# Forty small unread products ahead of the transposes of chunk 4's K, in a delta-rule attention and SwiGLU kernel

## The chip, the cores and the metric

The kernel runs on one core of one Trainium2 chip. The metric is the device time of one execution in microseconds; the time of a kernel is the median of its runs. The profile is of one execution, which has a time of its own and a span, from its first instruction to its last.

## What is computed

Two stages in float32, the second on the output of the first. The attention stage is a delta rule: for each of 4 batches and 8 heads, a 48x48 state is carried over 768 steps.

```
k_n = k / (norm(k) + 1e-6)
for t in range(S):
    y[t]  = q[t] @ state
    v_old = k_n[t] @ state
    state = state + beta[t] * outer(k_n[t], v[t] - v_old)
x   = y, heads side by side          # 3072 tokens x 384
g   = x @ w_gate                     # 384 x 1536
out = (g * sigmoid(g) * (x @ w_val)) @ w_out
```

## The kernel before

The sequence is cut into 12 chunks of 64 steps. Within a chunk the recurrence becomes matrix products: K is transposed (`turned`, from line 485), the products of K with itself and with Q are formed (`gram_steps`, L527), a triangular system is inverted for two chunks at a time (`invert`, `join`, L826 and L838 for the chunks 2 and 3, L921 and L935 for later pairs), and `advance` (L960 to L1212) uses these with the state: L977 and L960 multiply by the state, L1043 applies the inverse, L1145 updates the state, L1133 finishes y, L1206 transposes y for the next stage, and ScalarE copies that to SBUF at L1212. The feed-forward stage of a chunk works on its 256 tokens: gate and value products (L1409 for the chunks 0 and 1, L1313 for later ones, which use a scheme with fewer products), and the output products (L1436, L1519).

The order is written out by hand: all engines are under a manual schedule, and each engine's instructions run in the order in which the program issues them. The feed-forward products of chunk c are interleaved with the steps of the attention stage for chunk c+1: `point(c)` issues the next step of `advance`, or, through `prep_step`, the next preparation. One such preparation is `products(k_c, q_c)` (L1643), a generator of two steps. Its first step issues the transposes of K of chunk k_c and of Q of chunk q_c; its second issues their products. K of the chunks 4 and 5, and Q of chunk 2, are transposed on TensorE (L511, eight 128x128 transposes for each, into the PSUM pair `px` for K and `py` for Q) and copied out by ScalarE (L515). From chunk 6 on VectorE transposes K. The constant `AHEAD` is 4. `products(4, 2)` is issued right after the transposes of y of chunk 1 (L1206), which go to `py`.

There are already two kinds of product whose result nobody reads. `unread` (L651) is a 128x32 by 128x512 product; `small_unread` (L653 to L658) is a 32x32 by 32x1 product, in turn on the four 32-row quadrants. In the kernel before, 48 small ones and two large ones stand at the start, and 16 small ones (to `py`) and some large ones a little later, all before 26 us.

```
def small_unread(count, tag="px"):
    p = banks("p_t", tag)[0]
    for n in range(count):
        q_ = QUADS[n % 4][0]
        nc.tensor.matmul(p[q_, 0:1], half[q_], half[q_, 0:1])
```

In the trace each float32 product has two weight loads and two products, so 48 of these appear as 96 loads (PEld) and 96 products (PE). A transpose has one of each. Whatever TensorE executes is read from its own stream of instructions, which the profile lists as packets of queue q8.

Of the kernel before, what the change touches and what calls it, by code (L numbers as in the profile page):

```python
# [20 lines left out]
def kernel(  # L21
# [74 lines left out]
    AHEAD = 4  # L96
# [379 lines left out]
    def banks(name, tag):  # L476

        if type(tag) is int:
            return [ps_ffn([128, 512], name, tag + i) for i in range(2)]
        p = ps_pair(name, tag)  # L480
        return [p[:, 0], p[:, 1]]
# [3 lines left out]
    def turned(c, of_q, tag=None):  # L485

        if tag is None:
            tag = "py" if of_q else "px"
        x = qpad[c % QB] if of_q else kn_of(c)
        late = c >= blocks_of[of_q][1]  # L490
        if of_q:
            xt_v = qs_v[:, :, :, :, 0:C].rearrange("p b bp j i -> p bp j b i")
        elif late:
            xt_v = kt_of(c).rearrange("p (b bp j i) -> p bp j b i", bp=NB, b=2, j=NJ)
        else:
            xt_v = kt_of(c).rearrange("p (bp j b i) -> p bp j b i", bp=NB, j=NJ, b=2)
        (qt if of_q else kt)[c] = xt_v
        if late:
            blocks = blocks_of[of_q][2].rearrange("p bp h d -> p (bp h d)")
            if of_q:  # L500
                blocks = blocks.rearrange("p (u i) -> p u i", i=C)
            nc.vector.transpose(q_t if of_q else kt_of(c), blocks)
            spent.append(1.8)
            if c + 1 < NCH:
                late_loads.append(lambda: load_blocks(of_q, c + 1))
            return
        p_t = banks("p_t", tag)
        for bp in range(NB):
            for j in range(NJ):
                at = slice(128 * j, 128 * j + 128)  # L510
                nc.tensor.transpose(p_t[bp][:, at], x[:, bp, 2 * j : 2 * j + 2], ident)  # L511
            if type(tag) is int:
                nc.scalar.copy(xt_v[:, bp], p_t[bp].rearrange(P_T, j=NJ, b=2))
        for bp in range(NB if type(tag) is not int else 0):
            nc.scalar.copy(xt_v[:, bp], p_t[bp].rearrange(P_T, j=NJ, b=2))  # L515
        if of_q and c + QB < Q_BLOCKS:
            load_q(c + QB)
# [43 lines left out]
    def gram(*args):  # L561
        for _ in gram_steps(*args):
            pass
# [89 lines left out]
# [6 lines that stand above are left out]
# [983 lines left out]

    def products(k_c, q_c):  # L1643

        if k_c is not None:
            turned(k_c, False)
        if q_c is not None:
            turned(q_c, True)
        yield
        if k_c is not None:  # L1650
            gram(k_c, False, None, (nc.scalar.copy, nc.scalar.copy))
            if k_c % 2 == 1:
                fills.append((k_c // 2, invert(k_c // 2)))
        if q_c is not None and q_c < MERGED:
            gram(q_c, True)
        yield
# [30 lines left out]
    def prep_step(c):  # L1687

        for g in range(1, c // 2 + 2):
            late = g == 1 and (  # L1690
                hold or steps("join", g) >= 2 and steps("advance", 2) < 4
            )
            if g in inverted and steps("join", g) < (4 if g == 1 else 2) and not late:
                step("join", join if g > 1 else join_1, *((g,) if g > 1 else ()))
                return True
        if going:
            next(going.pop())
            return True
        k_c, q_c = None, None
        if q_of and steps("advance", q_of[0] - 1) >= 3:  # L1700
            q_c = q_of.pop(0)
        elif not (c > 0 and hold and not todo and k_ready()):
            return False
        if k_ready():
            k_c = k_of.pop(0)
        gen = products(k_c, q_c)
        next(gen)
        if k_c is not None or q_c < MERGED:
            going.append(gen)
        return True  # L1710
# [210 lines left out]
```

## Time and profile before

| what | value |
|---|---|
| median of 3 runs | 694.35 us (692.88, 694.35, 695.93) |
| profiled execution, its time | 693.74 us |
| profiled execution, its span | 692.0 us |
| TensorE busy (PE) | 676.7 us, 98% of the span, 10756 products |
| weight loads (PEld) | 631.0 us, 91%, 10756 loads |
| VectorE, ScalarE, GpSimdE busy | 60%, 38%, 27% |
| mean granted TensorE clock | 0.995 |
| DMA | 62.23 MB, mean 90 GB/s |

How to read it: "busy" counts a product from its start to its modelled end, so a stream of small products that overlap counts as busy all through. The granted clock is the share of full speed that TensorE was given. In the timeline each row is a group of like instructions: its start in us from the start of the span, its length in us, the engine, the line, the operation, what is written and read, the count, and in brackets how long the engine sat idle before it and what ended that. "issue" in a bracket is idle time in which the engine waited for no other engine and no transfer of data that the profile shows. The chain is the sequence of work that ended last, followed back from the last instruction.

### The profile page before, as it was taken

How to read it: one execution, taken by the hardware profiler on the slowest of the kernel's cores; microseconds unless marked ns; L12 is line 12 of the kernel's file. 1: busy time of each engine (PE TensorE's matmuls, PEld its weight loads, DVE VectorE, ACT ScalarE, POOL GpSimd, SP SyncE). 2: the span in 40 equal slices, each digit the busy share in tenths (PEclk: the TensorE clock that was granted, in tenths of full speed). 3: DMA queues.
4: the chain of work that ended last, by engine and by line, in shares of the span. 5: the costliest groups of instructions: out<-in, count | busy, mean ns of one | idle time of the engine just before them, and what ended most of it. 6: DMA issues, size and time to landing. Idle time of an engine off the chain costs nothing.

```text
span 692.0 us, 24441 instructions
## 1 busy us (share of the span) xinstructions
PE 676.7 (98%) x10756; PEld 631.0 (91%) x10756; DVE 415.8 (60%) x874; ACT 262.7 (38%) x557; POOL 189.9 (27%) x310
## 2 busy tenths in 40 slices
PE   8889999999999999999999999999999999999997
PEld 5777888666999999999899999999999999999997
DVE  7887688897567565637457646655555534433342
ACT  5776765124432522344233245232144242142230
POOL 5110032007880318810036830308810000000000
PEclk9999999999999999999999999999999999999999
DMA  9678733026550611564422364243143121221210
GB/s 138 155 184 223 208 127 103 12 40 182 119 113 15 133 48 41 109 123 69 94 71 71 70 129 81 56 98 82 54 109 69 56 63 47 56 62 46 70 46 23
DMA packets 143849, 62.23 MB, mean 90 GB/s; under 512 B 122976, under 2 KB 126048, under 8 KB 143744
## 3 DMA queue, kind: packets, MB, share of 16 engines
q1 hardware_dynamic: 141536, 60.19, 37.6%
q8 instruction: 84, 1.38, 0.8%
q10 hardware_dynamic: 2080, 0.39, 0.4%
q14 instruction: 21, 0.17, 0.1%
q0 software_dynamic: 128, 0.10, 0.1%
HBM read 53.58 MB, written 7.08 MB: 88 GB/s over the span
## 4 chain that ended last, share of the span: by engine, by line
PE 89%; DMA 4%; ACT 2%; SPq 2%; issue 1%; DVE 1%; POOL 0%; DVEq 0%; POOLq 0%; ACTq 0%
PE ffn L1313 43%; PE ffn L1519 20%; PE ffn L1409 8%; PE ffn L1436 4%; DMA h_f<-in_moe_w_val_dram 2%; PE p_px L977 2%; PE p_py L960 2%; PE p_px L1043 2%; PE p_py L1133 2%; PE p_px L1145 1%; SPq L140 1%; PE p_px L527 1%; PE p_py L1206 1%; PE p_py L935 1%; PE p_px L921 1%
## 5 line engine op out<-in xcount | busy, mean ns | idle before, releaser
L1313 PE MATMUL ffn<-x_ffn,wg_sb 128*128 128x128 f32 x840 | 129.2, 277 | 0.5 <-ACT ffn L1369 0.3
L1313 PE MATMUL ffn<-x_ffn,wv_sb 128*128 128x128 f32 x840 | 128.6, 276 | 0.0
L1313 PEld LDWEIGHTS ffn<-x_ffn,wg_sb 128*128 128x128 f32 x840 | 112.0, 193 | 1.0 <-ACT ffn L1369 0.7
L1313 PEld LDWEIGHTS ffn<-x_ffn,wv_sb 128*128 128x128 f32 x840 | 111.1, 193 | 0.0
L1348 DVE TENSOR_TENSOR h_f<-sil,ffn 128x256 f32<-128x256 f32 x120 | 49.8, 418 | 84.4 <-ACT sil L1343 83.0
L1343 ACT ACTIVATE sil<-ffn 128x256 f32<-128x256 f32 x120 | 45.8, 383 | 129.7 <-PE ffn L1313 128.9
L1519 PE MATMUL ffn<-wo_sb,h_f 128*128 128x192 f32 x480 | 83.4, 328 | 0.0
L860 POOL TENSOR_TENSOR n_b<-mb,half 128x32 f32<-128x32 f32 x5 | 30.0, 6006 | 181.9 <-DVE mb L569 181.9
L1519 PEld LDWEIGHTS ffn<-wo_sb,h_f 128*128 128x128 f32 x480 | 78.1, 190 | 0.3
L605 POOL TENSOR_TENSOR zb<-zb,tmp 128x31 f32<-128x31 f32 (+15 forms) x124 | 71.0, 573 | 9.7
L599 POOL TENSOR_TENSOR tmp<-zb,mb 128x31 f32<-128x31 f32 (+15 forms) x124 | 65.9, 532 | 16.9 <-DVE mb L586 7.5
L1480 DVE TENSOR_TENSOR ffn<-ffn,p_sb 128x512 f32<-128x512 f32 x58 | 40.4, 696 | 49.1 <-ACT ffn L1369 47.6
L1313 PE MATMUL ffn<-x_t,h_f 128*128 128x128 f32 x480 | 61.0, 280 | 0.2 <-ACT ffn L1326 0.2
L1313 PEld LDWEIGHTS ffn<-x_t,h_f 128*128 128x128 f32 x480 | 56.3, 192 | 2.1 <-ACT ffn L1326 0.4
L1480 DVE TENSOR_TENSOR o_sb<-o_sb,ffn 128x192 f32<-128x192 f32 x49 | 17.3, 352 | 63.5 <-PE ffn L1519 60.9
L1326 ACT COPY ffn<-ffn 128x512 f32<-128x512 f32 x30 | 17.1, 571 | 60.8 <-PE ffn L1313 60.8
L1477 DVE TENSOR_TENSOR h_f<-h_f,h_f 128x256 f32<-128x256 f32 x60 | 30.3, 510 | 11.7 <-PE ffn L1519 10.5
L1519 PE MATMUL ffn<-last_k,h_f 128*128 128x192 f32 x200 | 36.0, 327 | 0.0
L1409 PE MATMUL ffn<-x_ffn,wg_sb 128*128 128x256 f32 x144 | 34.4, 385 | 0.3 <-DVE x_ffn L1210 0.3
L1409 PE MATMUL ffn<-x_ffn,wv_sb 128*128 128x256 f32 x144 | 34.7, 389 | 0.0
L1519 PEld LDWEIGHTS ffn<-last_k,h_f 128*128 128x128 f32 x200 | 32.9, 190 | 0.1
L1409 PEld LDWEIGHTS ffn<-x_ffn,wv_sb 128*128 128x128 f32 x144 | 27.5, 193 | 3.8
(323 smaller groups left out, 1121.3 us busy)
## 6 DMA issues: line engine op xcount, KB each, us to landing
h_f<-w_s SPq DMA_DIRECT2D x60, 256.0 KB, 2.9
p_sb<-w_s SPq DMA_DIRECT2D x27, 256.0 KB, 2.7
vin<-in_v_dram SPq DMA_DIRECT2D x48, 96.0 KB, 3.2
out_dram<-o_sb SPq DMA_DIRECT2D x48, 96.0 KB, 2.2
kn<-in_k_dram SPq DMA_DIRECT2D x20, 192.0 KB, 4.8
zt<-in_moe_w_out_dram SPq DMA_DIRECT2D x6, 384.0 KB, 4.2
qpad<-in_q_dram SPq DMA_DIRECT2D x36, 64.0 KB, 3.1
w_s<-h_f SPq DMA_DIRECT2D x7, 256.0 KB, 3.5
```

What stands on the lines that cost most here:

```text
L599: engine.tensor_tensor(out=t_v, in0=zb[:, 0 : j + 1, j : j + 1].to_broadcast([128, j + 1, m]), in1=mb[:, j : j + 1, j + 1 : R].to_broadcas ...
L605: engine.tensor_tensor(out=zb[:, 0 : j + 1, j + 1 : R], in0=zb[:, 0 : j + 1, j + 1 : R], in1=t_v, op=ALU.add,)
L860: nc.gpsimd.tensor_tensor(out=n, in0=mb.rearrange("p j i -> p (j i)")[:, 0 : R * R : R + 1], in1=half, op=ALU.pow,)
L1313: nc.tensor.matmul(p[:, u], w(u), moving, start=start and u == 0, stop=True, skip_group_check=True,)
L1326: nc.scalar.copy(p_y, p_x)
L1343: nc.scalar.activation(sil[:, n].rearrange("p (i n) -> p i n", i=2), p[:, 0:2], ACTF.Silu)
L1348: nc.vector.tensor_tensor(out=h_of(c, f, j), in0=sil[:, n].rearrange("p (i n) -> p i n", i=2), in1=p[:, 2:4], op=ALU.mult,)
L1409: nc.tensor.matmul(ps[name][:, i], w_sb[:, t, (f + i) * 128 : (f + i + 1) * 128], xts[c][:, t], start=(t == 0 and i == 0), stop=(t == KT - 1),
L1436: nc.tensor.matmul(p_o, hs[c, f - f % 2][:, f % 2, bp * 128 : (bp + 1) * 128], wo_sb[:, f], start=(f == 0), stop=(f == FT - 1),)
L1477: nc.vector.tensor_tensor(out=out, in0=a, in1=b, op=ALU.subtract)
L1480: nc.vector.tensor_tensor(out=out, in0=a, in1=b, op=ALU.add)
L1519: nc.tensor.matmul(p[x, part], a(f - f % 2)[:, f % 2], b(f), start=not begun and f == 0, stop=f == FH - 1, skip_group_check=True,)
```

## The change

One call is added to the first step of `products`; nothing is taken away, and no other line is changed.

```
     def products(k_c, q_c):
 
+        if k_c == AHEAD:
+            small_unread(40)
         if k_c is not None:
             turned(k_c, False)
         if q_c is not None:
             turned(q_c, True)
         yield
```

The condition holds once, for chunk 4. The 40 products write to column 0 of the first bank of `px`, which the transposes of K overwrite right after. They stand in TensorE's order between the six transposes of y of chunk 1 (L1206) and the eight transposes of K of chunk 4 (L511). In the program as built, TensorE has 40 products more, 80 records of loads and 80 of products in the trace, and as many semaphore instructions as before; the wait on VectorE, for the last reader of `px`, moves from the first transpose of K to the first small product, and the waits for the loads of K stay at the transpose. The other four engines have the same instructions in the same order.

More of the change, by code (lines that the diff above doesn't have):

```diff
@@ L1643, in products @@
     def products(k_c, q_c):
+        if k_c == AHEAD:
+            small_unread(40)
         if k_c is not None:
```

## The prediction

> **What bounds the kernel now.** I read the chain of waits first. TensorE has 89% of it, and 1% is "issue", time in which nothing visible held the engine.
>
> ```profile
> q8 instruction: 84, 1.38, 0.8%
> ...
> PE 89%; DMA 4%; ACT 2%; SPq 2%; issue 1%; DVE 1%; POOL 0%; DVEq 0%; POOLq 0%; ACTq 0%
> ```
>
> Then the timeline of PE where the products go in, between L1206 and the first L511:
>
> ```profile
> 66.26 0.88 PE L1206 MATMUL p_py<-ident,y 128*128 128x128 f32 x6
> 66.97 1.04 PE L511 MATMUL p_px<-ident,kn 128*128 128x128 f32 x8
> 68.43 1.09 PE L511 MATMUL p_py<-ident,qpad 128*128 128x128 f32 x8 [0.42 <-ACT x_ffn L1212]
> 69.36 2.75 PE L1409 MATMUL ffn<-x_ffn,wg_sb 128*128 128x256 f32 x12
> ```
>
> The eight transposes of K run without a wait. Those of Q wait for ScalarE, which must empty `py` (L1212); between the last start for K (67.73) and the first load for Q (68.43) lie 0.69 us where 0.11 is the usual step. So some 0.6 us of added work is covered here.
>
> Then every "issue" gap inside a run of like products, in timelines of PE. This carries the forecast.
>
> ```profile
> 14.32 0.35 PE L658 MATMUL p_py<-half 32*32 32x1 f32 x21
> 15.73 0.28 PE L658 MATMUL p_py<-half 32*32 32x1 f32 x11 [1.06 <-issue]
> ```
> ```profile
> 159.74 0.90 PE L1043 MATMUL p_px<-vin,zt 64*64 64x48 f32 x42
> 160.88 0.56 PE L1043 MATMUL p_px<-vin,zt 64*64 64x48 f32 x22 [0.24 <-issue]
> ...
> 163.61 0.76 PE L1133 MATMUL p_py<-uu,p_sb 64*64 64x48 f32 x38
> 165.15 0.61 PE L1133 MATMUL p_py<-uu,p_sb 64*64 64x48 f32 x26 [0.79 <-issue]
> ```
> ```profile
> 241.43 1.10 PE L935 MATMUL p_py<-t,z 32*32 32x32 f32 x107
> 243.44 0.38 PE L935 MATMUL p_py<-t,z 32*32 32x32 f32 x21 [0.91 <-issue]
> ```
> ```profile
> 338.48 1.20 PE L935 MATMUL p_py<-t,z 32*32 32x32 f32 x119
> 341.06 0.27 PE L935 MATMUL p_py<-t,z 32*32 32x32 f32 x9 [1.38 <-issue]
> ```
>
> Each cuts a run of identical products in two, so no data is at fault. Count all TensorE records of the trace (loads, products, semaphores) from zero: the first record after each gap is number 705, 5313, 5569, 8385, 11713. The differences are 18, 1, 11 and 13 times 256. Queue q8 moved 84 packets, 1.38 MB, for 21,636 records: 16,384 bytes, or 256 records of 64 bytes, each. So TensorE runs out of code at a block's edge, in the records 193, 449, 705, ... Ahead of the gap at 339.68 the packet ran from 338.63 to 339.58 and PE resumed at 341.06, 1.47 after; at the others 1.36 to 1.49 (1.41 at 243.43). Over the later blocks a packet starts about 1.05 us after the sequencer (some 44 records ahead of PE) passes an edge when DMA is quiet, up to 4.1 when it is full, and takes 0.9 to 1.5. So a block that PE finishes within about 3.4 us (quiet) to 6 us (full) makes it wait.
>
> One further loss follows the longest gap. The windows view (columns: stretch, its length, PE busy and products, granted clock, DMA share, GB/s):
>
> ```profile
> 338.30:341.70 3.40, 2.02 (x134) 1.00 0.62 88
> 341.70:345.10 3.40, 3.40 (x18) 0.50 0.61 104
> 345.10:348.50 3.40, 3.40 (x35) 1.00 0.04 13
> ```
>
> After 3.4 us in which PE was busy for 2.02, the clock is halved for 3.4 us: about 1.7 us of work lost. (The other halved stretch, 51.50 to 55.00, lies ahead of the change.)
>
> **The change, part by part.** *The products.* 80 records. At the start 96 loads lie within 1.34 us, 14 ns each; of the run at 14.32, 22 loads lie within 0.16 us, 7.4 ns each. So 0.6 to 1.1 us; I take 0.85, since the full-clock row is the nearer but short. One edge (record 3521) now falls in them: its packet ended at 65.85, so with 1.36 the code is there at 67.21, and the small products reach it at about 67.1: 0.1 more. The first transpose moves from 66.86 by about 1.0, the Q transposes by 0.4 once the 0.6 of cover is used. From there the chain goes over L1409, L1420 and the conversions on VectorE back to TensorE at 77.84; all of it hangs on TensorE, so the delay stays: **+0.4** (0.05 to 0.7). ScalarE copies K (L515, 68.91) some 0.3 later and catches up before L1418 waits for PE at 72.15. The wait for the last reader of `px` (L1154, over at 64.72) holds nothing.
>
> The Trainium skill ("TensorE: Matmul & The Clock Gate", "Wait — 56ns, not 53.3ns?") says that starts of products never come closer than about 25 ns; by it the 80 records would take an estimated 2.0 us and the sum would be 1.2 higher. The rows above, 7 to 14 ns apart, speak against it.
>
> *The edges.* The 80 loads and 80 products are 160 records, and the count of semaphore records is the same. So every later edge falls 160 records earlier in the code: at old records 33, not 193, modulo 256. All four late gaps lose their cause. Neighbours start 15 ns apart but a product's record lasts 0.22, so a gap costs its idle time plus 0.2; from start to start they are 0.46, 1.01, 1.10 and 1.57: **-4.1**. The halved clock at 341.7 goes with the longest: **-1.7**. Bounds: none of it gone (0) to all (-5.8). I take all, since at the new places near 242 and 340 a block has over 4 us.
>
> *The new edges.* I listed the old time of each record that is 33 modulo 256 and compared each block's time with what its fetch needs. Most have room, as the old ones had; four places do not. (1) 150.8 to 154.0, 3.2 us of L826, L1436 and L838, DMA half full: 0 to 1.0, say 0.4. (2) 154.0 to 157.6, 3.6 us: 0 to 1.4, say 0.3. (3) 163.1 to 168.2, 4.1 us without the old gap, with DMA full (0.96 of 163 to 169, 351 GB/s); the old packet asked for at 165.15 started only at 169.30: 0 to 2.4, say 0.9. (4) 255.7 to 257.8 and 396.1 to 398.1, 2.1 us, but asked for 2.4 us ahead under L1313: 0 to 0.5 each, say 0.3 together. **+1.9** (0 to 5.8).
>
> What is late after a gap goes? TensorE itself: from 175 to 690 it is busy all but about 5 us, and VectorE has 60% and ScalarE 38% of the span. Nothing else on the path takes over.
>
> **Sum.** +0.4 - 4.1 - 1.7 + 1.9 = -3.5, against the profiled execution's own 693.74 us (span 692.0 and 1.7 around it): 690.2. I say **690.4**, a little up for a chance that a new gap at (3) halves a clock of its own. The profiled run is 0.6 below the median of the three (694.35), so against that median it is -0.6%, just beyond the 0.5% that a measurement of this kernel can tell from no change.
>
> **Rivals.** *The gaps only move.* The new places cost what the old did, with a halved clock among them: 693.74 + 0.4 = 694.1 (693 to 695.5). For it: code still comes just in time, and fast blocks remain; against: fast blocks cut at other places mostly have 4 to 6 us.
>
> *Code is no limit.* If the gaps have another cause that stays with their products, only the work counts: 693.74 + 0.4 = 694.1 too. Against it: the steps of 256. The Trainium skill ("Runtime: NRT & Kernel Launch", "Instruction fetch mechanics") states this rule, that code comes in 16 KiB blocks of 256 instructions and that the cost of crossing an edge is mostly hidden. The trace agrees on the blocks, not on the hiding.
>
> *Place (3) starves long.* If its packet too starts only at about 169, as the old one did, the block comes at 171.5 in place of 168.2, 3.5 us late; a window of 3.4 us with PE busy under about 2 then halves the clock: 1.7 more. If the halved clock near 341 also appears after another gap and (1) and (2) cost their most (2.4), the sum is 693.74 + 0.4 - 4.1 + 3.5 + 1.7 + 2.4 = 697.6. It decides the sign when the packet of (3) starts later than about 168.5. For it: the full DMA there; against: the old packet at 162.87, asked for at 160.75 in half-full DMA, took 2.1 us.
>
> **How the numbers follow.** Forecast 0.56 (own range 688.6 to 692.3; 0.46 of it faster by over 0.5%, 0.10 within), the gaps only move 0.17 (0.15 within, 0.02 slower), code no limit 0.14 (within), place (3) 0.13 (0.02 within, 0.11 slower). Faster 0.46, within 0.41, slower 0.13. The range 688.8 to 695.0 leaves out some 0.05 below and 0.13 above.
>
> **What would show it.** In the trace after: L658 at about 66.9 as 80 records in 0.6 to 1.2 us; the Q transposes 0.05 to 0.7 later; no "issue" gap within L1043, L1133 (160 to 165) or L935 (243, 341), and any new one at a record that is 193 modulo 256 in the new count; full clock around 342. Gaps left in their old products would refute the edges; gaps of 1 us or more at the four places would mean that I priced them too low.

## The result, and the profile after

The changed kernel takes 691.57 us (median of 21 runs, 688.89 to 693.55), the kernel before 693.31 (21 runs, 691.15 to 695.93). The ratio is 0.9972, 95% interval 0.9961 to 0.9984: faster by 0.3%, 1.9 us by the ratio and 1.7 us between the medians. The profiled execution after took 691.39, with a span of 689.7.

The page of the changed kernel, sections 3 and 4: one packet of code more, and TensorE still has nine tenths of the chain.

```profile
q8 instruction: 85, 1.39, 0.9%
...
PE 90%; DVE 3%; DMA 3%; ACT 2%; issue 1%; SPq 1%; POOL 0%; DVEq 0%; ACTq 0%; POOLq 0%
```

The timeline of PE at the place of the change:

```profile
65.86 0.87 PE L1206 MATMUL p_py<-ident,y 128*128 128x128 f32 x6
66.66 0.95 PE L658 MATMUL p_px<-half 32*32 32x1 f32 x80
68.89 1.07 PE L511 MATMUL p_px<-ident,kn 128*128 128x128 f32 x8 [1.28 <-DMA kn<-in_k_dram]
69.79 1.85 PE L511 MATMUL p_py<-ident,qpad 128*128 128x128 f32 x8
71.44 3.66 PE L1409 MATMUL ffn<-x_ffn,wg_sb 128*128 128x256 f32 x12
```

The 80 products of the trace take 0.95 us, as forecast (0.6 to 1.1). Two things were not forecast: TensorE then waits for K of chunk 4, and the transposes of Q and the first L1409 are stretched (1.85 for 1.09, 3.66 for 2.75). The windows view (columns: stretch, its length, PE busy and products, granted clock, DMA share, GB/s) says why: a halved clock.

```profile
66.30:69.85 3.55, 2.27 (x93) 1.00 0.86 249
69.90:73.25 3.35, 3.35 (x14) 0.50 1.11 241
```

The four late places, in the timeline of PE after:

```profile
163.18 1.15 PE L1043 MATMUL p_px<-vin,zt 64*64 64x48 f32 x64
164.26 1.56 PE L1436 MATMUL ffn<-wo_sb,h_f 128*128 128x384 f32 x4
165.75 0.94 PE L1145 MATMUL p_px<-uu,kn 64*48 64x48 f32 x64
166.50 1.11 PE L1133 MATMUL p_py<-uu,p_sb 64*64 64x48 f32 x64
```
```profile
243.26 1.29 PE L935 MATMUL p_py<-t,z 32*32 32x32 f32 x128
```
```profile
339.20 1.29 PE L935 MATMUL p_py<-t,z 32*32 32x32 f32 x128
```

Each run of like products is whole again: x64 where it was x42 and x22 or x38 and x26, x128 where it was x107 and x21 or x119 and x9. The clock around 342 is full:

```profile
338.30:341.70 3.40, 3.40 (x148) 1.00 0.90 159
341.70:345.10 3.40, 3.40 (x33) 1.00 0.56 105
```

One new gap stands where place (1) was, at record 5057 (193 modulo 256 in the new count), inside L838:

```profile
156.89 0.39 PE L838 MATMUL p_py<-t,p_sb 32*32 32x32 f32 x6
157.52 0.18 PE L838 MATMUL p_py<-t,p_sb 32*32 32x32 f32 x1 [0.24 <-issue]
```

### The profile page after: what moved, and what is told of

It reads as the page before. It is cut to its first block, busy times and chain, and to the rows that moved or that the text cites. A ratio compares the mean times of both kernels' runs of the same rounds, so it can differ in the third digit from the quotient of the medians.

```text
span 689.7 us, 24601 instructions
## 1 busy us (share of the span) xinstructions
PE 675.9 (98%) x10836; PEld 630.4 (91%) x10836; DVE 414.6 (60%) x874; ACT 263.2 (38%) x557; POOL 192.4 (28%) x310
## 4 chain that ended last, share of the span: by engine, by line
PE 90%; DVE 3%; DMA 3%; ACT 2%; issue 1%; SPq 1%; POOL 0%; DVEq 0%; ACTq 0%; POOLq 0%
PE ffn L1313 43%; PE ffn L1519 20%; PE ffn L1409 8%; PE ffn L1436 4%; PE p_px L977 2%; DMA kn<-in_k_dram 2%; PE p_py L960 2%; PE p_px L1043 2%; PE p_py L1133 1%; PE p_px L1145 1%; PE p_px L527 1%; PE p_py L1206 1%; PE ffn L1072 1%; DMA wo_sb<-in_moe_w_gate_dram 1%; PE p_px L921 1%
## 5 line engine op out<-in xcount | busy, mean ns | idle before, releaser
L1313 PEld LDWEIGHTS ffn<-x_ffn,wg_sb 128*128 128x128 f32 x840 | 111.1, 192 | 1.0 <-ACT ffn L1369 0.7
L1313 PEld LDWEIGHTS ffn<-x_ffn,wv_sb 128*128 128x128 f32 x840 | 110.7, 192 | 0.0
L599 POOL TENSOR_TENSOR tmp<-zb,mb 128x31 f32<-128x31 f32 (+15 forms) x124 | 68.7, 554 | 16.9 <-DVE mb L586 7.5
L1409 PE MATMUL ffn<-x_ffn,wg_sb 128*128 128x256 f32 x144 | 35.3, 392 | 0.3 <-DVE x_ffn L1210 0.2
L1409 PE MATMUL ffn<-x_ffn,wv_sb 128*128 128x256 f32 x144 | 33.8, 382 | 0.0
L1409 PEld LDWEIGHTS ffn<-x_ffn,wg_sb 128*128 128x128 f32 x144 | 27.4, 196 | 4.8 <-DVE wg_sb L309 0.8
```

Source lines behind the costliest of these rows:

```text
L599: engine.tensor_tensor(out=t_v, in0=zb[:, 0 : j + 1, j : j + 1].to_broadcast([128, j + 1, m]), in1=mb[:, j : j + 1, j + 1 : R].to_broadcas ...
L1313: nc.tensor.matmul(p[:, u], w(u), moving, start=start and u == 0, stop=True, skip_group_check=True,)
L1409: nc.tensor.matmul(ps[name][:, i], w_sb[:, t, (f + i) * 128 : (f + i + 1) * 128], xts[c][:, t], start=(t == 0 and i == 0), stop=(t == KT - 1),
```

## The experiments

All counts of records are TensorE's. For every profile I split the time at four records: the first weight load of L1206 in chunk 1, the first load of L1409 after the transposes, the first load of L826 after that, and a record near the end (21,600 in the count of before; "the end" below). Experiments that move the edges after 114 have the edges of their own count.

| kernel | records added, place | L1206 to L1409, us | L1409 to L826, us | L826 to the end, us | clock halved between 65 and 77 |
|---|---|---|---|---|---|
| before, first profile | none | 2.99 | 81.21 | 534.54 | no |
| before, second profile | none | 4.20 | 81.21 | 533.77 | no |
| changed, first | 160, chunk 4's K | 5.36 | 82.22 | 529.25 | yes |
| changed, second | 160, chunk 4's K | 6.50 | 81.75 | 530.05 | yes |
| changed, third | 160, chunk 4's K | 3.93 | 81.31 | 529.59 | no |
| e1_64 | 256, chunk 4's K | 6.80 | 81.27 | 533.33 | yes |
| e2_16 | 64, chunk 4's K | 5.77 | 81.87 | 529.86 | yes |
| e3_k5 | 160, chunk 5's K | 4.71 | 82.34 | 530.78 | no |
| e4_start | 160, start | 2.98 | 81.21 | 530.48 | no |
| e5_16_k5 | 64, chunk 5's K | 4.35 | 81.72 | 530.22 | no |
| e6_dense | 64, chunk 4's K, 8 of them large | 4.69 | 81.21 | 530.34 | no |
| e7_40_dense | 160, chunk 4's K, 8 of them large | 5.07 | 81.21 | 529.67 | no |
| e8_1043 | 176, L1043 of chunk 1 | 2.98 | 81.57 | 529.76 | no |

The fifth column is the study in short: 533.3 to 534.5 wherever the late edges are those of before, 529.3 to 530.8 wherever they are moved, however and wherever that is done. The 534.5 of the first profile holds a halved clock near 342; the 533.3 and 533.8 do not.

My theory A was the prediction's: the gain comes from where the edges of the code blocks fall. Rival B: the delay, or the products, at this place bring it. Rival C: code is no limit.

**A whole block of 256 records (e1_64).**

```
         if k_c == AHEAD:
-            small_unread(40)
+            small_unread(64)
```

> 64 small products at the same place in place of 40: 256 records, one whole code block, so every later edge falls on the same instruction as in the kernel before. Theory A (the gain of 40 comes from where the edges of the code blocks fall): gaps again at 160.6, 164.4, 242.5 and 339.7 of the old trace (shifted by under 2 us), no gain, only the work of 128 records: 0.6 to 1.5 us slower than before, ratio 1.001 to 1.002. Theory B (the delay or the small products at this place themselves bring the gain, by letting transfers or other engines get ahead): more products, at least the gain of 40, ratio 0.997 or less, and the four gaps gone. Theory C (code is no limit, the difference between 40 and none is not due to the edges): ratio of 40 plus some 0.5 us, 0.998.

Measured: ratio 1.0048 (1.0027 to 1.0070), slower. Its timeline of PE:

```profile
163.90 0.90 PE L1043 MATMUL p_px<-vin,zt 64*64 64x48 f32 x42
165.06 0.56 PE L1043 MATMUL p_px<-vin,zt 64*64 64x48 f32 x22 [0.27 <-issue]
...
167.79 0.76 PE L1133 MATMUL p_py<-uu,p_sb 64*64 64x48 f32 x38
169.62 0.61 PE L1133 MATMUL p_py<-uu,p_sb 64*64 64x48 f32 x26 [1.06 <-issue]
```
```profile
246.23 1.10 PE L935 MATMUL p_py<-t,z 32*32 32x32 f32 x107
248.51 0.38 PE L935 MATMUL p_py<-t,z 32*32 32x32 f32 x21 [1.18 <-issue]
```
```profile
343.56 1.20 PE L935 MATMUL p_py<-t,z 32*32 32x32 f32 x119
345.62 0.27 PE L935 MATMUL p_py<-t,z 32*32 32x32 f32 x9 [0.86 <-issue]
```

The runs are cut after the very same products, 42, 38, 107 and 119, as in the kernel before. Rivals B and C are out: the same products at the same place, more of them, and nothing is gained. Its cost was 3.3 us in place of 0.6 to 1.5, a miss of the size; part is seen at the place itself, where the profile has a halved clock and, with 256 records added, a second edge, at record 3777, whose gap cuts the transposes of Q (seven, 0.73 us idle, one).

**Sixteen products (e2_16)**, `small_unread(16)` at the same place.

> 16 small products at the same place: 64 records, edges at records 129 modulo 256 of the old count. Theory A: of the blocks cut there, my count finds one that is short of time, near 405 (about 0.5 us), and the four old gaps go (4.1 us by the profiled run of before); the 64 records take 0.25 to 0.9 us beside a cover of 0.6: ratio 0.993 to 0.996, better than 40. Theory B: less than half the delay, so less of the gain: 0.998 to 1.000. Theory C: 1.000.

Measured: 0.9958 (0.9937 to 0.9979), at the slow end of A's range. In its profile the clock is halved at the place. Gaps from start to start: 0.69 at L1133 (165 in the old time), 0.45 at L1133 near 211; the one that I had counted near 405 did not appear.

**Another place (e3_k5)**: the 40 products ahead of chunk 5's K, where PE is busy without a pause.

```
-        if k_c == AHEAD:
+        if k_c == AHEAD + 1:
             small_unread(40)
```

> The 40 products stand ahead of the transposes of chunk 5's K instead (near 114 in the old trace), where PE runs densely and nothing covers them: the edges after that place are as with 40 at chunk 4. Theory A: late gaps as in the changed kernel (one of about 0.5 us near 154), 0.6 to 1.1 us of work in full, none of the changed kernel's loss near 70 (a wait for K and a halved clock, 1.3 and 1.7 us in its profiled run, if these come from the products): ratio 0.995 to 0.998. Theory B: the place is gone, and with it the gain: 1.001 to 1.002.

Measured: 0.9972 (0.9954 to 0.9989), the ratio of the changed kernel. B falls a second time. Its gaps were 0.52 at 300.8 and 1.19 at 395.1, the second at place (4) of the prediction, the first at an edge that I had thought to have room. TensorE waits for K of chunk 4 here too, 2.16 us, with no product at that place.

**At the start (e4_start)**, `small_unread(88)` in place of 48.

> The 40 products stand at the very start instead (88 in place of 48), where TensorE waits for the first K anyway; all edges of the program move by 160 records. Theory A: late gaps as in the changed kernel; the edges before 66 move too, with new gaps of up to 1 to 3 us near 12, 19 and 22 in place of that of 1.1 us at 14.7, in a stage in which TensorE mostly waits for loads and vector work: ratio 0.996 to 1.001. Theory B: no product near chunk 4's K, no gain: 1.000.

Measured: 0.9988 (0.9969 to 1.0007), which A and B both allow; the late stage tells them apart, since it gains as the others do (530.48). Where the rest of the gain went is not shown. Chunk 1's L1206 starts at 68.41, against 66.26 before, and the edges ahead of it have gaps of 1.96 us at record 1217 and 1.76 at 1729; but in the eleven profiles whose code up to there is that of before, that start varies from 65.30 to 69.20.

**The kernel before, a second profile.**

> The kernel before again, for a second look at it. Theory A (edges): gaps of 0.2 to 1.6 us after the records 5313, 5569, 8385 and 11713, 2.5 to 4.5 us in all from start to start. For the place of the products: in three of the other four profiles K of chunk 4 landed at 68.2 to 70.1, later than TensorE wanted it; if that is the usual case and the first profile of before was lucky, L511 waits here too, by 1 to 2.4 us, without any product added. If the wait for K is an effect of the products, it is absent here. No halved clock between 65 and 75.

Measured, in its timeline of PE:

```profile
66.31 0.88 PE L1206 MATMUL p_py<-ident,y 128*128 128x128 f32 x6
68.83 1.06 PE L511 MATMUL p_px<-ident,kn 128*128 128x128 f32 x8 [1.65 <-DVE wo_sb L289]
69.73 1.04 PE L511 MATMUL p_py<-ident,qpad 128*128 128x128 f32 x8
```

The second transfer of K landed at 68.70, and TensorE went on at 68.83, so the wait is for K, not for the VectorE instruction that the bracket names. This execution took 694.23 us. Without any added product TensorE waits 1.65 us here. K landed between 66.9 and 70.1 in all twelve other profiles and at 65.70 only in the one I predicted from. The four late gaps are there again: 0.76, 1.28, 1.65 and 1.09 from start to start, 4.8 us (4.1 in the first). The halved clock near 342 is not.

**The changed kernel, a second and a third profile.**

> The changed kernel again, for a second look. Theory A: no gap at the four old places, one of about 0.5 us at record 5057. At the products: a wait for K of chunk 4 of up to 1.5 us, and, if small products do not count as work for the clock gate, the clock halved for 3.4 us between 67 and 75 again (it was in all three profiles with small products there, and in none of the three without); if the halving was chance, not.

> The changed kernel a third time, timed on the same chip as the two below. Its profile: the clock halved for 3.4 us between 67 and 75, as in its first two; no gap at the four old places; K of chunk 4 lands at 67 to 70, so L511 or the edge inside the small products holds TensorE until then. Ratio 0.996 to 0.999.

The timed ratio of the third is 0.9971 (0.9954 to 0.9989). Their timelines of PE at the place, the second first:

```profile
70.00 0.30 PE L658 MATMUL p_px<-half 32*32 32x1 f32 x16
72.15 0.79 PE L658 MATMUL p_px<-half 32*32 32x1 f32 x64 [1.85 <-issue]
72.88 1.54 PE L511 MATMUL p_px<-ident,kn 128*128 128x128 f32 x8
```
```profile
66.73 0.30 PE L658 MATMUL p_px<-half 32*32 32x1 f32 x16
67.53 0.70 PE L658 MATMUL p_px<-half 32*32 32x1 f32 x64 [0.49 <-issue]
68.16 1.09 PE L511 MATMUL p_px<-ident,kn 128*128 128x128 f32 x8
```

The edge at record 3521 falls after 16 of the 80 products, and TensorE waits for code there, for 1.85 and 0.49 us. After the first of these waits the clock is halved, after the second not. The windows view of the second and the third profile:

```profile
69.90:73.30 3.40, 1.55 (x86) 1.00 1.10 176
73.40:76.75 3.35, 3.35 (x16) 0.50 0.98 241
```
```profile
65.40:68.80 3.40, 2.77 (x94) 1.00 0.95 291
68.80:72.20 3.40, 3.40 (x24) 1.00 1.17 211
```

So the clock was halved in two of the three profiles, and my expectation for the third missed. The second of these executions took 696.21 us, more than the kernel before: besides the wait of 1.85 us and the halved clock here, its attention stage came to L1206 only at 69.20, after two halved stretches, at 18.8 and 59.7.

**Sixteen products at chunk 5's K (e5_16_k5)**, to see what the halved clock costs.

> 16 small products ahead of the transposes of chunk 5's K. Edges after 114 as with 16 at chunk 4 (one or two gaps, 0.5 to 1.2 us in all). Theory A with a halved clock caused by the products at chunk 4: the work of 64 records (0.25 to 0.5 us) uncovered, but no halved clock near 70: ratio 0.993 to 0.996, by up to 1.5 us better than 16 at chunk 4. If the halving there is chance or covered: as 16 at chunk 4, 0.995 to 0.997. Theory B (the place brings the gain): 1.000.

Measured: 0.9979 (0.9958 to 1.0000). The clock is not halved near 70, yet the time is not better than with 16 at chunk 4; a miss. From L1206 to L826 the profile is 1.6 us shorter than that of e2_16 (86.1 against 87.6), but three late gaps are left, 0.62, 0.73 and 0.45 us from start to start, 1.8 in all where I had counted 0.5 to 1.2.

**Dense work in place of small products (e6_dense, e7_40_dense).** Two large unread products join 14 small ones (64 records in all) or 38 (160 records, the changed kernel's edges).

```
         if k_c == AHEAD:
-            small_unread(40)
+            unread(2)
+            small_unread(14)
```

This is e6_dense; e7_40_dense has 38 small ones.

> At chunk 4's K, two large unread products (128x32 by 128x512, 8 records, 1.7 us) and 14 small ones (56 records): 64 records in all, so the edges of 16 small ones. If the halved clock near 70 comes from a lack of dense work, it is gone here (1.7 us gained), at a cost of 0 to 1.2 us as K is late or early: ratio 0.993 to 0.996. If small products have no part in the halving, the clock is halved here too or the added 1.7 us of work shows in full: 0.996 to 0.999.

> At chunk 4's K, two large unread products and 38 small ones: 160 records, so exactly the edges of the changed kernel. If the halved clock near 70 is due to small products standing where dense work is short, it is gone: 1.7 us less, and the large products' 1.7 us lie mostly beside the wait for K: 0.5 to 1.7 us faster than the changed kernel on the same chip, ratio to before 0.993 to 0.996. If the halving costs nothing outside the profile, or is chance: as the changed kernel or up to 1 us slower, 0.997 to 0.999.

Measured: 0.9961 (0.9945 to 0.9977), on the border of its two expectations, and 0.9983 (0.9965 to 1.0001). In both profiles the clock stays full near 70. The windows view of e6_dense:

```profile
66.50:69.90 3.40, 3.39 (x42) 1.00 1.00 267
69.90:73.30 3.40, 3.40 (x25) 1.00 1.09 239
```

But e7_40_dense, timed on the same chip as the changed kernel, is not faster than it (691.30 against 690.99). I had expected 0.5 to 1.7 us of gain, so this missed. Its timeline of PE at the place:

```profile
68.28 1.91 PE L651 MATMUL p_px<-half 128*32 128x512 f32 x4
70.11 0.80 PE L658 MATMUL p_px<-half 32*32 32x1 f32 x76
70.85 1.09 PE L511 MATMUL p_px<-ident,kn 128*128 128x128 f32 x8
```

K landed at 68.88, so only the first 0.6 us of the added products lies beside the wait for K; the rest, about 2 us, holds the transposes up, and what is saved on the clock is spent there. In e6_dense K landed at 69.17, and the transposes start at 69.50. How often the clock is halved in executions that are not profiled stays open.

**Where TensorE waits anyway (e8_1043)**: 44 products ahead of the inverse's product in chunk 1, to `py`.

```
+        if c == 1:
+            small_unread(44, "py")
         for bp, j, par, b, first in every():
```

> 44 small products (176 records) ahead of the application of the inverse in chunk 1 (L1043, near 48), to the py banks, where TensorE waits 0.6 to 1.7 us for VectorE in every profile so far. All later edges move by 176 records: by my count of blocks one or two gaps of 0.4 to 0.5 us near 154 and 157 are left, none at the four old places, and the one near 57 (L1097, 0.7 to 2.3 us) goes. The clock may be halved near 52, in a stage that waits for loads and vector work anyway; no products near 70, so no halving there. Theory A: 0.991 to 0.995, the best so far. Theory B (the place ahead of chunk 4's K brings the gain): 1.000.

Measured: 0.9958 (0.9943 to 0.9974); 689.89 us against 690.99 for the changed kernel on the same chip. It is faster than the kernel before; that it beats the changed kernel by 0.16% is within the intervals. It gained less than the 0.5% to 0.9% expected: gaps of 0.63 and 0.45 are left near 155.5 and 159.7, as counted, and one of 0.84 is new at 51.9.

## Why the prediction was right or wrong

*The edges: right.* The gaps of the kernel before come from running out of code at every 256th record; all four went as the count was shifted by 160, and came back when it was shifted by 256. The prediction's three late terms, -4.1, -1.7 and +1.9, make -3.9; from L826 to the end the two first profiles differ by 5.3 (534.54 to 529.25), the second of before and the third of the changed kernel by 4.2.

*The late halved clock: right for one profile only.* It was in the profile I predicted from and not in the second one of before. Near 342 the gap was 1.09 there, against 1.57; and the 1.65 at record 8385 halved no clock, so the length of a gap alone does not decide it. I took a term as typical that was not: where the clock is not halved, the term of -1.7 has nothing to give.

*The new edges: mis-sized, too dear in the changed kernel.* Forecast +1.9. Place (1) cost 0.45, 0.61 and under 0.35 in the three profiles of the changed kernel (0.4 forecast); place (2) 0.45 in the second; place (3), for which I had put 0.9, nothing in any; place (4) 0.83 in the third, at the second of its two blocks. Together 0.5 to 1.1. In three experiments with the same late edges (e7_40_dense, e3_k5, e4_start) the late gaps are 1.0, 1.7 and 1.9, so the forecast is the upper end rather than out of reach; 0.5 of the 1.7 lies at an edge that was not on my list. Place (3) is quiet in all six. In the first profile of the changed kernel its packet ran from 167.47 to 168.75, and TensorE came to the block at 170.22 without a gap. That (3) stays quiet refutes the step "the old packet asked for at 165.15 started only at 169.30" as a measure for a packet asked for two microseconds earlier; its rival (3.5 us there) is out.

*The step that failed is "+0.4 (0.05 to 0.7)" for the products.* From L1206 to L826 the changed kernel took 87.6, 88.3 and 85.2 us, the kernel before 84.2 and 85.4. Against the second profile of before, that is +2.2, +2.9 and -0.2; the term was +0.4. Two things in the step were wrong, and a third was too small:

- "The Q transposes by 0.4 once the 0.6 of cover is used." The cover that counts is the wait for K, 1.65 us in the second profile of before. The first showed no wait because K had landed early, at 65.70. In three of the six profiles that have no product at this place TensorE waits for K, for 1.65, 1.80 and 2.16 us; in the other three K is there in time. So the work itself is free where K is late, which I did not see, having one profile in hand.
- Nothing was put down for the clock. In the profile windows of 3.41 us, after which it is halved near 70, the full-size products (L1409, L1206, L511, L651) cover 1.25 and 0.61 us in the changed kernel, 1.42 in e1_64 and 1.21 in e2_16. In the windows that hold the place in the other profiles, and after which it is not halved, they cover 1.76 us or more. The small unread products add to "busy" without making up for them. It is not a matter of full size alone: in e4_start a window just ahead of the place, filled with 64x48 products, holds only 1.05 us of full-size ones, and in the first profile of the changed kernel the window from 28.89 to 32.30, busy for 2.10 us, holds none, only 64x48 products of L1043 and L1072; the clock stays full after both. The cost of the halved clock is part of the 2.2 and 2.9 us.

The edge at record 3521, put down for 0.1, held TensorE for 0.49 and 1.85 us in the third and the second profile. In the third, K landed only at 67.70, so a part of the 0.49 would have been spent on the wait for K. So the place cost 2 to 3 us in two of the three profiles and nothing in the third.

*The sum.* A late gain of 4 to 5 and a loss of 0 to 3 at the place fit what the timed runs show, 1.7 to 1.9 us. The forecast of 3.3 (690.4 against 693.74) has the right sign and the right mechanism for the late edges; its late gain and its loss at the place are both too small, and that the two errors in part cancel is luck. Faster by over 0.5%, to which I gave the largest chance, did not come: the gain is 0.3%. The profiled run of before lies 0.4 above the median of 21 runs, so against that median 690.4 would be a gain of 2.9.

*The rivals.* "The gaps only move" and "code is no limit" both said 694.1; both fall with the fifth column of the table. What the Trainium skill ("Runtime: NRT & Kernel Launch", "Instruction fetch mechanics") says of 16 KiB blocks agrees with the 16,384 bytes of each packet; that their crossing is mostly hidden holds for most of the 85 here, and not for some of those in or right behind runs of 64x48 or 32x32 products that follow each other 15 ns apart.

## What to carry to other kernels

When a run of identical small products is cut by an "issue" gap, count the records of TensorE up to it; if the gaps lie at one remainder of 256, a few cheap records ahead of them move all later edges, and a full 256 are the test. Put them where TensorE waits anyway and where other products are not already few, since here a stretch with few of them halved the clock for the next 3.4 us. One profile is one draw: a wait that it does not show (K here) or a halved clock that it does show may be the exception, so price such terms by how often they would occur.

## What the runs showed of the hardware that was not expected

Small unread products count as busy in the profile and, as far as these profiles show, hardly as work for the clock. A window of 3.4 us that was busy for 2.73 us (e1_64) was followed by a halved clock, and one with 2.00 us of busy time, all of it in full-size products (e3_k5), was not. The windows views, e1_64 first:

```profile
66.00:69.40 3.40, 2.73 (x137) 1.00 0.73 175
69.45:72.80 3.35, 3.17 (x15) 0.50 1.02 304
```
```profile
64.05:67.45 3.40, 2.00 (x12) 1.00 1.02 197
67.45:70.85 3.40, 2.51 (x20) 1.00 0.93 314
```

The same holds over the thirteen profiles, cut into windows of 3.41 us from each start of full clock and up to 680 us. Without the products of L658, every window with 1.42 us of busy time or less, ten of them, is followed by a halved clock. Of the windows with more, three are (1.80, 1.86 and 2.04 us, none with a product of L658), and others from 1.53 us on are not. With L658 counted the two kinds overlap far more: halved after up to 2.75 us (the e1_64 window above, to its exact ends), not halved after 1.67. What sets the limit between 1.5 and 2.0 us is not shown.

And the length of a wait for code varies from run to run at the same edge, with nothing changed: 0.46 and 0.76 at record 5313, 1.01 and 1.28 at 5569, 1.10 and 1.65 at 8385, 1.57 and 1.09 at 11713, in two executions of the kernel before.
